# Value pooling as one VectorE reduction, and ScalarE work half a step later, in an attention + MoE + MoE kernel

## Chip, cores and metric

One core of a Trainium2 chip runs the whole program. The metric is the device time of one execution in microseconds (us). TensorE, VectorE, ScalarE, GpSimd and SyncE are called PE, DVE, ACT, POOL and SP in the rows, and PEld is TensorE's loading of weights.

## What is computed

Attention with pooled keys and values, then a gated MLP, then a routed mixture of eight experts. The part that the change touches is the attention and the first pieces of the MLP:

```python
B, H, S, D = 8, 8, 576, 64; pool = 8; Sp = S // pool              # 72 keys a head
k_p = k.reshape(B, H, Sp, pool, D).mean(axis=3)
v_p = v.reshape(B, H, Sp, pool, D).mean(axis=3)
scores = np.matmul(q, k_p.transpose(0, 1, 3, 2)) / np.sqrt(D)
attn = softmax(scores)
x = np.matmul(attn, v_p)                                           # tokens x 512 after a transpose
x = (silu(x @ w_gate) * (x @ w_val)) @ w_out                       # 512 -> 1536 -> 512
...                                                                # then 8 experts, top 1
```

## The kernel before

The kernel is written with a scheduling layer: functions issue instructions, and the layer decides, engine by engine, in which order they stand. What the author sets is a key for each piece of work (`at_key(key, function, ...)`); the pieces are called in the order of their keys, and the layer prefers earlier ones, but it moves instructions between pieces where it expects an engine to wait. The order that stands in the built program is therefore shown below apart from the diff.

**Attention stage (about the first 270 us).** There are 36 steps x of 128 query rows, nine for each pair of batches. For a step, `st_scores` makes scores on TensorE (sc), VectorE takes row maxima (nm, L335) and ScalarE the exponentials (e, L339). `st_norm` sums them on VectorE (sm, L345), adds a small number on GpSimd (L346), takes the reciprocal on VectorE (L347) and scales e on GpSimd (L348). `st_aT` transposes e on TensorE (aTp, L365) and copies it to `at`. There are four e tiles, e_100 to e_103, used in turn. `st_av` multiplies `at` with the pooled values vb on TensorE (xp, L380), ScalarE copies xp to xs (L382), and when four pairs of heads are done xs is stored to DRAM (xT).

**Pooling.** `k_pool` sums groups of eight keys by one VectorE reduction (kp, L294); the keys lie with the pool innermost. `v_pool` (L304) sums groups of eight values on GpSimd by three additions over 4, 2 and 1 of the eight, with the feature innermost; `v_finish` (L310, GpSimd) masks the result (vsum) by head into vb. Raw keys and values have two buffers each and are loaded by SP's queue, so a load waits until the pooling of two batches earlier is done.

**Units.** Parts of the MLP fill TensorE during attention. A unit u is 256 tokens; `u_load` reads them back from xT (ur), splits them into a high half (uh, ScalarE L217) and a low half (ul, GpSimd L218). `u_gemm1(u, f)` does 24 matmuls (ugv, L233), then tanh on ScalarE (ut, L236), two products on VectorE (L237, L238), a rounding on ScalarE (uhh, L241) and a difference on VectorE (uhl, L242). `u_gemm2` multiplies these by the output weights (acc, L253). There are 12 units with two f each. xp and ugv take their PSUM banks from one pair of buffers ("xg").

**Weights.** `w_split` (L143 to L157, ScalarE and VectorE) splits the first six weight tiles during the first 45 us. `load_bias` (L171 to L179, VectorE) runs once in the middle of the stage.

After the attention stage TensorE runs the MLP's matmuls (gv L457, x L480) and then the experts (L761, L780).

Of the kernel before, what the change touches and what calls it, by code (L numbers as in the profile page):

```python
# [8 lines left out]
F32 = mybir.dt.float32  # L9
# [4 lines left out]
ALU = mybir.AluOpType  # L14
AX = mybir.AxisListType
# [3 lines left out]
B, H, S, D = 8, 8, 576, 64  # L19
NT, DM, FF = B * S, H * D, 1536  # L20
E, F2 = 8, 1024
POOL = 8
# [49 lines left out]
def attention_moe_moe2(ctx: ExitStack, tc: tile.TileContext, q, k, v, w_gate, w_val, w_out,  # L72
                       modality, w_gate2, mbias, w12, consts, out):
    nc = tc.nc
    sy, gp, ve, ac, pe = nc.sync, nc.gpsimd, nc.vector, nc.scalar, nc.tensor
# [7 lines left out]
    def bank(tag, name):  # L83
        n = {"s": 2, "x": 4, "y": 2, "sc": 2, "at": 2, "xg": 2, "acc": 2}[tag]
        return psp[0].tile([128, 512], F32, tag=tag, bufs=n, name=name)
# [114 lines left out]
    ue = {}  # L200
# [22 lines left out]
    def u_gemm1(u, f):  # L223
        hi, lo = ue[u]["x"]
        w = wgv[f]
        p = bank("xg", "ugv")
        o = [p[:, 0:256], p[:, 256:512]]
        for j in range(2):
            n = 0
            for kk in range(4):  # L230
                ws = slice(j * 512 + kk * 128, j * 512 + (kk + 1) * 128)
                for a, x in ((0, hi), (0, lo), (1, hi)):
                    pe.matmul(o[j], lhsT=w[:, a, ws], rhs=x[kk], start=n == 0, stop=n == 11)  # L233
                    n += 1
        t = m1.tile([128, CH], F32, tag="t", bufs=2, name="ut")[:, 0:256]
        ac.activation(out=t, in_=o[0], func=ACTF.Tanh, scale=0.5)  # L236
        ve.scalar_tensor_tensor(out=t, in0=t, scalar=1.0, in1=o[0], op0=ALU.add, op1=ALU.mult)  # L237
        ve.tensor_tensor(out=t, in0=t, in1=o[1], op=ALU.mult)  # L238
        hh = m1.tile([128, CH], F32R, tag="hh", bufs=2, name="uhh")[:, 0:256]
        hl = m1.tile([128, CH], F32R, tag="hl", bufs=2, name="uhl")[:, 0:256]  # L240
        ac.copy(hh, t)  # L241
        ve.tensor_tensor(out=hl, in0=t, in1=hh.bitcast(F32), op=ALU.subtract)  # L242
        ue[u][f] = (hh, hl)
# [21 lines left out]
    with tc.tile_pool(name="p0", bufs=1) as p0, tc.tile_pool(name="ps0", bufs=1, space=PSUM) as ps0:  # L265
        psp[0] = ps0
        NE = 4
        vs_t = [p0.tile([128, 5, 64], F32, name=f"vsum{i}") for i in range(2)]
# [5 lines left out]
        for t in e_t:  # L274
            gp.memset(t[:, 576:640], 0.0)

        k_raw, v_raw, vb_t, q_t, at_t, xs_t, nm_t, sm_t = {}, {}, {}, {}, {}, {}, {}, {}

        def q_load(b):
            q_t[b] = p0.tile([128, 4, S], F32, tag="q", bufs=2, name="qt")  # L280
# [4 lines left out]
            sy.dma_start(out=k_raw[b].rearrange("p k r -> p (k r)"), in_=k[b])  # L285

        def v_load(b):
            v_raw[b] = p0.tile([128, 5, POOL, 64], F32, tag="vraw", bufs=2, name="vraw")
            sy.dma_start(out=v_raw[b].rearrange("p c r d -> p (c r d)"), in_=v[b])

        def k_pool(b):
            raw = k_raw.pop(b)
# [5 lines left out]
                              func=ACTF.Copy, scale=1.0 / 64)  # L298

        def v_pool(b):  # L300
            t = v_raw.pop(b)
            for w in (4, 2, 1):
                o = t[:, :, 0:w] if w > 1 else vs_t[b % 2].unsqueeze(2)
                gp.tensor_tensor(out=o, in0=t[:, :, 0:w], in1=t[:, :, w:2 * w], op=ALU.add)  # L304

        def v_finish(b):
            vb = p0.tile([128, 4, 2, 2, 64], F32, tag="vb", bufs=2, name="vb")
# [64 lines left out]

        def st_av(b, half, hp):
            n = 256 + 64 * half
            if hp == 0:
                xs_t[b, half] = p0.tile([128, 4, 320], F32, tag="xs", bufs=2, name="xs")
            xs = xs_t[b, half]
            xp = bank("xg", "xp")
            for w in range(2):
                pe.matmul(xp[:, :n], lhsT=vb_t[b][:, hp, w, :], rhs=at_t[b, half][:, hp + w, :], start=w == 0,  # L380
                          stop=w == 1)
            ac.copy(xs[:, hp, :n], xp[:, :n])  # L382
            if hp == 3:
                c0 = (b % 2) * S + half * 256
                ac.dma_start(out=xT_d[b // 2][:, :, c0:c0 + n], in_=xs[:, :, :n])
# [3 lines left out]
        def at_key(key, fn, *args):  # L389
            ev_.append((key, len(ev_), fn, args))  # L390

        as_, an, av, avs = 3.0, 1.7, 0.7, 0.45
        WS0, WSK, U0, UK = -3.9, 1.0, 5.0, 1.3
# [4 lines left out]
        for g in range(4):  # L398
            for b in (2 * g, 2 * g + 1):
                x = 9 * g + (4 if b % 2 else 0) - as_ - 1.0  # L400
                at_key(x, k_pool, b)
                at_key(x - 4.0, k_load, b)
                at_key(x - 3.9, q_load, b)
                x0 = 9 * g + (6 if b % 2 else 1) + av
                at_key(x0 - 1.5, v_finish, b)
                at_key(x0 - 3.0, v_pool, b)
                at_key(x0 - 5.5, v_load, b)
                x1 = 9 * g + (8 if b % 2 else 4) + av
                for hp in range(4):
                    at_key(x0 + hp * avs, st_av, b, 0, hp)  # L410
                    at_key(x1 + hp * avs, st_av, b, 1, hp)
        for n in range(3 * NW1 + 4):
            at_key((-7.8, -7.7, -5.0, -4.5)[n] if n < 4 else WS0 + (n - 4) * WSK + 0.1, w_load, n)
        for n in range(3 * NW1):
            at_key(WS0 + n * WSK, w_split, n)
        uitems = [(u, f) for u in range(NU) for f in range(EF)]
        def stored(i):
            return 9 * (i // 9) + (1, 1, 4, 4, 6, 6, 8, 8, 8)[i % 9] + av + 3 * avs

        x = U0 - UK  # L420
        for n, (u, f) in enumerate(uitems):
            x += UK
            if f == 0:
                xl = max(x - 1.7, stored(2 * u + 1) + 0.5)
                x = max(x, xl + 1.5)
                at_key(xl, u_load, u)
            if n == 8:
                at_key(xl - 0.1, load_bias, p0)
            at_key(x, u_gemm1, u, f)
            at_key(x + 0.9 * UK, u_gemm2, u, f)  # L430
        at_key(34.0, x_load, ORDER[0])
        at_key(36.0, x_load, ORDER[1])
# [492 lines left out]
```

## Time and profile before

| | |
|---|---|
| median of three runs | 1573.29 us (1572.08 to 1575.23) |
| the profiled execution | 1572.41 us |
| its span in the profile | 1570.5 us (1.9 us lie around it) |
| TensorE busy in the span | 1507.6 us, 96% |
| VectorE, ScalarE, GpSimd busy | 958.2, 644.1, 230.2 us |

TensorE is busy for 96% of the span, so a reader looks for the 4% where it is not, and for stretches in which its granted clock is below the full one.

### The profile page before, as it was taken

The numbers are of one execution on the slowest core, as the hardware profiler recorded it, in microseconds if no ns is written. First come the engines' busy times: TensorE is split into PE (matmuls) and PEld (weight loads), VectorE is DVE, ScalarE is ACT, GpSimd is POOL, SyncE is SP. The second block draws the span as 40 slices with busy tenths as digits, with TensorE's granted clock in tenths as the row PEclk, the third lists the DMA queues.
The fourth block names the chain that finished last, engine by engine and source line by source line (L and its number), as shares of the span: only waits on it lengthen the run. The fifth ranks groups of instructions, "written<-read, shape, count | busy, mean of one in ns | idle before, by whom it ended". The sixth has DMA issues, their size and how long they took to land. (4 is left out here: it accounts for less than half of the span.)

```text
span 1570.5 us, 23370 instructions
## 1 busy us (share of the span) xinstructions
PE 1507.6 (96%) x8664; PEld 1369.3 (87%) x8664; DVE 958.2 (61%) x2280; ACT 644.1 (41%) x1469; POOL 230.2 (15%) x249
## 2 busy tenths in 40 slices
PE   4788999999999999999999999999999999999996
PEld 3577888899999999999999999998888898988985
DVE  7556444699385763755736637277986666665660
ACT  4545766555422121121221211123556666656651
POOL 4676543000000000000000000001031211211101
PEclk9899999999999999999999999999999999999998
DMA  7686433444110301101011010007477666666520
GB/s 300 254 278 215 139 121 125 150 154 133 51 41 21 91 11 54 58 11 51 28 44 51 11 51 31 1 21 269 141 239 260 219 234 224 209 225 229 186 97 28
DMA packets 62219, 198.50 MB, mean 126 GB/s; under 512 B 7021, under 2 KB 28177, under 8 KB 49298
## 3 DMA queue, kind: packets, MB, share of 16 engines
q1 hardware_dynamic: 44114, 161.78, 30.8%
q0 software_dynamic: 6080, 19.42, 3.5%
q10 hardware_dynamic: 11904, 15.73, 2.8%
q8 instruction: 70, 1.15, 0.3%
q14 instruction: 51, 0.42, 0.1%
HBM read 162.28 MB, written 35.15 MB: 126 GB/s over the span
## 5 line engine op out<-in xcount | busy, mean ns | idle before, releaser
L457 PE MATMUL gv<-xh,gv 128*128 128x384 f32 x2048 | 546.5, 338 | 0.8 <-DVE t L462 0.8
L457 PEld LDWEIGHTS gv<-xh,gv 128*128 128x128 f32 x2048 | 373.4, 188 | 6.7 <-DVE t L462 1.2
L457 PE MATMUL gv<-xl,gv 128*128 128x384 f32 x1024 | 345.9, 338 | 0.0
L761 PEld LDWEIGHTS hp<-x2hl,w 128*128 128x128 f32 x1824 | 233.5, 188 | 10.9
L761 PE MATMUL hp<-x2hl,w 128*128 128x256 f32 x1824 | 242.5, 281 | 0.0
L480 PE MATMUL x<-wo,hh 128*128 128x512 f32 x768 | 242.1, 396 | 0.0
L457 PEld LDWEIGHTS gv<-xl,gv 128*128 128x128 f32 x1024 | 192.4, 188 | 5.2
L780 PE MATMUL po<-w,hh 128*128 128x512 f32 x608 | 193.1, 399 | 2.4 <-ACT hh L765 2.4
L510 DVE CUSTOM_DVE_ANT_0 junk<-row,w2g 128x512 bf16<-128x512 f32 x288 | 184.8, 682 | 1.6 <-ACT row L501 1.5
L461 ACT ACTIVATE t<-gv 128x384 f32<-128x384 f32 x128 | 63.1, 493 | 290.1 <-PE gv L457 290.0
L655 POOL DMA_INDIRECT xg<-x2d,gidx x38 | 39.5, 1039 | 953.9 <-DVE oidx L642 816.9
L732 DVE TENSOR_TENSOR w<-raw,w 128x512 fp32r<-128x512 f32 x152 | 106.1, 698 | 116.8 <-ACT w L730 112.8
L462 DVE SCALAR_TENSOR_TENSOR t<-t,gv 128x384 f32<-128x384 f32 x128 | 70.5, 551 | 171.8 <-ACT t L461 171.6
L480 PEld LDWEIGHTS x<-wo,hh 128*128 128x128 f32 x768 | 143.2, 189 | 23.5
L466 ACT CAST hh<-t 128x384 fp32r<-128x384 f32 x128 | 65.7, 513 | 235.2 <-DVE t L463 235.0
L480 PE MATMUL x<-wo,hl 128*128 128x512 f32 x384 | 152.4, 397 | 0.0
L730 ACT CAST w<-raw 128x512 fp32r<-128x512 f32 x152 | 94.1, 619 | 135.4 <-PE po L780 123.3
L780 PE MATMUL po<-w,hl 128*128 128x512 f32 x304 | 121.5, 400 | 0.1
L780 PEld LDWEIGHTS po<-w,hh 128*128 128x128 f32 x608 | 103.3, 188 | 16.7 <-ACT hh L765 2.6
L463 DVE TENSOR_TENSOR t<-t,gv 128x384 f32<-128x384 f32 x128 | 70.5, 551 | 54.7 <-PE gv L457 54.5
L734 DVE TENSOR_TENSOR w<-raw,w 128x512 fp32r<-128x512 f32 x152 | 103.7, 682 | 0.0
L467 DVE TENSOR_TENSOR hl<-t,hh 128x384 fp32r<-128x384 f32 x128 | 70.9, 554 | 39.9 <-ACT hh L466 39.7
(144 smaller groups left out, 1892.1 us busy)
## 6 DMA issues: line engine op xcount, KB each, us to landing
raw<-in_moe_w_dram SPq DMA_DIRECT2D x76, 1024.0 KB, 5.7
vraw<-in_v_dram SPq DMA_DIRECT2D x8, 1280.0 KB
x2d<-row SPq DMA_DIRECT2D x36, 256.5 KB, 3.4
kraw<-in_k_dram SPq DMA_DIRECT2D x8, 1152.0 KB, 5.9
qt<-in_q_dram SPq DMA_DIRECT2D x8, 1152.0 KB
xr<-xT SPq DMA_DIRECT2D x48, 192.0 KB, 2.4
w2g<-in_moe_w_gate_dram SPq DMA_DIRECT2D x12, 512.0 KB, 8.1
w2g<-in_moe_w_val_dram SPq DMA_DIRECT2D x12, 512.0 KB, 3.4
```

Source lines behind the costliest of these rows:

```text
L457: pe.matmul(p, lhsT=w[:, a, ws], rhs=x[kk], start=n == 0, stop=n == 11)
L462: ve.scalar_tensor_tensor(out=t, in0=t, scalar=1.0, in1=o[0], op0=ALU.add, op1=ALU.mult)
L463: ve.tensor_tensor(out=t, in0=t, in1=o[1], op=ALU.mult)
L466: ac.copy(hh, t)
L467: ve.tensor_tensor(out=hl, in0=t, in1=hh.bitcast(F32), op=ALU.subtract)
L480: pe.matmul(o, lhsT=hx[:, ts], rhs=w[:, f % 2, a, :], start=f == f0 and n == 0, stop=f == NF - 1 and n == 2)
L510: ve.tensor_tensor_reduce(out=junk, in0=r[:, 0:DM], in1=w2g[:, e, :], scale=1.0, scalar=0.0, op0=ALU.mult, op1=ALU.add, accum_out=L[:, tt, ...
L730: ac.copy(h1, src)
L732: ve.tensor_tensor(out=w[:, 1, 0:512].rearrange("p (k f) -> p k f", k=4), in0=src, in1=h1.bitcast(F32), op=ALU.subtract)
L734: ve.tensor_tensor(out=w[:, 1, 512:1024], in0=w2s, in1=w[:, 0, 512:1024].bitcast(F32), op=ALU.subtract)
L761: pe.matmul(hp, lhsT=w[:, a, c0:c0 + 128], rhs=x[:, kk, :], start=n == 0, stop=n == 11)
L780: pe.matmul(b["po"][tt], lhsT=hx[:, ts], rhs=w[:, a, 512:1024], start=f == 0 and n == 0, stop=f == 7 and n == 2)
```

## The change

It has two parts. `v_pool` becomes one VectorE reduction for each batch, over values which the host now lays out with the pool of eight innermost; the load moves the same bytes in rows of the same length. And the ScalarE work (with the VectorE work that follows it) of a unit and of xs gets functions and keys of its own: `u_act` stands 0.4 of a unit's pitch behind `u_gemm1`, and `st_xs` 0.3 of a step behind `st_av`; the reading back of tokens (`stored`) moves by the same 0.3.

```diff
@@ u_gemm1
+        ue[u]["o"] = o
+
+    def u_act(u, f):
+        o = ue[u].pop("o")
         t = m1.tile([128, CH], F32, tag="t", bufs=2, name="ut")[:, 0:256]
         ac.activation(out=t, in_=o[0], func=ACTF.Tanh, scale=0.5)
         ve.scalar_tensor_tensor(out=t, in0=t, scalar=1.0, in1=o[0], op0=ALU.add, op1=ALU.mult)
@@ v_load
-            v_raw[b] = p0.tile([128, 5, POOL, 64], F32, tag="vraw", bufs=2, name="vraw")
+            v_raw[b] = p0.tile([128, 5 * 64, POOL], F32, tag="vraw", bufs=2, name="vraw")
@@ v_pool
-            t = v_raw.pop(b)
-            for w in (4, 2, 1):
-                o = t[:, :, 0:w] if w > 1 else vs_t[b % 2].unsqueeze(2)
-                gp.tensor_tensor(out=o, in0=t[:, :, 0:w], in1=t[:, :, w:2 * w], op=ALU.add)
+            ve.tensor_reduce(out=vs_t[b % 2].rearrange("p c d -> p (c d)"), in_=v_raw.pop(b), op=ALU.add, axis=AX.X)
@@ st_av
-            xp = bank("xg", "xp")
-            for w in range(2):
-                pe.matmul(xp[:, :n], lhsT=vb_t[b][:, hp, w, :], rhs=at_t[b, half][:, hp + w, :], start=w == 0,
-                          stop=w == 1)
-            ac.copy(xs[:, hp, :n], xp[:, :n])
+            xp = xp_t[b, half, hp] = bank("xg", "xp")
+            for w in range(2):
+                pe.matmul(xp[:, :n], lhsT=vb_t[b][:, hp, w, :], rhs=at_t[b, half][:, hp + w, :], start=w == 0,
+                          stop=w == 1)
+
+        def st_xs(b, half, hp):
+            ...
+            ac.copy(xs[:, hp, :n], xp_t.pop((b, half, hp))[:, :n])
@@ keys
+                    at_key(x0 + hp * avs + 0.3, st_xs, b, 0, hp)
+                    at_key(x1 + hp * avs + 0.3, st_xs, b, 1, hp)
@@ stored
-            return 9 * (i // 9) + (1, 1, 4, 4, 6, 6, 8, 8, 8)[i % 9] + av + 3 * avs
+            return 9 * (i // 9) + (1, 1, 4, 4, 6, 6, 8, 8, 8)[i % 9] + av + 3 * avs + 0.3
@@ units
             at_key(x, u_gemm1, u, f)
+            at_key(x + 0.4 * UK, u_act, u, f)
             at_key(x + 0.9 * UK, u_gemm2, u, f)
```

On GpSimd, about the eighth step (the second e_103) and the second batch's values, before:

```order
L348 TENSOR_TENSOR e_101<-e_101,sm 128x576
L346 TENSOR_SCALAR sm<-sm 128x8
L348 TENSOR_TENSOR e_102<-e_102,sm 128x576
L304 TENSOR_TENSOR vraw<-vraw 128x5x256
L346 TENSOR_SCALAR sm<-sm 128x8
L304 TENSOR_TENSOR vraw<-vraw 128x5x128
L348 TENSOR_TENSOR e_103<-e_103,sm 128x576
L304 TENSOR_TENSOR vsum_97<-vraw 128x320
L310 TENSOR_TENSOR vb<-vsum_97,cc 128x4x128
```

and now:

```order
L349 TENSOR_TENSOR e_101<-e_101,sm 128x576
L218 TENSOR_TENSOR ul<-ur,uh 128x256 x2
L311 TENSOR_TENSOR vb<-vsum_97,cc 128x4x128 x2
L347 TENSOR_SCALAR sm<-sm 128x8
L349 TENSOR_TENSOR e_102<-e_102,sm 128x576
L347 TENSOR_SCALAR sm<-sm 128x8
L349 TENSOR_TENSOR e_103<-e_103,sm 128x576
```

The three additions are gone from between the scalings of e; the first unit's ul and the second batch's vb now stand ahead of the scaling of e_102, where they stood behind e_103.

On VectorE at the same place (line numbers of the changed file are higher by one to four), before:

```order
L335 TENSOR_REDUCE nm<-sc 128x4
L345 TENSOR_REDUCE sm<-e_101 128x8
L335 TENSOR_REDUCE nm<-sc 128x4
L347 RECIPROCAL sm<-sm 128x8
L369 COPY at_341<-aTp 128x64
L369 COPY at_441<-aTp 128x64
L294 TENSOR_REDUCE kp<-kraw 128x288
L335 TENSOR_REDUCE nm<-sc 128x4 x2
L345 TENSOR_REDUCE sm<-e_102 128x8
```

and now:

```order
L298 TENSOR_REDUCE kp<-kraw 128x288
L336 TENSOR_REDUCE nm<-sc 128x4 x2
L346 TENSOR_REDUCE sm<-e_101 128x8
L370 COPY at_337<-aTp 128x64
L370 COPY at_437<-aTp 128x64
L348 RECIPROCAL sm<-sm 128x8
L305 TENSOR_REDUCE vsum_97<-vraw 128x320
L336 TENSOR_REDUCE nm<-sc 128x4 x2
L346 TENSOR_REDUCE sm<-e_102 128x8
```

The key reduction kp moved ahead of the maxima nm and of the sum for e_101, and the new value reduction vsum stands ahead of the next maxima and of the sum for e_102.

On ScalarE, around the first xs of the first batch, before:

```order
L382 COPY xs<-xp 128x256
L371 COPY at_341<-aTp 128x4x128
L156 CAST gv_218<-wa 128x512
L339 ACTIVATE e_100<-sc,nm 128x72 x8
L382 COPY xs<-xp 128x256 x2
L156 CAST wo_183<-wa 128x512
L382 COPY xs<-xp 128x256
L339 ACTIVATE e_101<-sc,nm 128x72 x8
```

and now:

```order
L386 COPY xs<-xp 128x256 x2
L372 COPY at_337<-aTp 128x4x128
L156 CAST gv_216<-wa 128x512
L340 ACTIVATE e_100<-sc,nm 128x72 x8
L386 COPY xs<-xp 128x256 x2
L389 DMA xT_66<-xs 512x1x256
L156 CAST wo_183<-wa 128x512
L340 ACTIVATE e_101<-sc,nm 128x72 x8
```

Two copies to xs stand together ahead of e_100's exponentials instead of one, and the store follows the fourth copy at once. Behind the attention stage the order on all engines is the same as before.

## Rows read from the trace of the kernel before

**Rows 1.** The page: busy us of each engine, share of the span, instructions.

```profile
PE 1507.6 (96%) x8664; PEld 1369.3 (87%) x8664; DVE 958.2 (61%) x2280; ACT 644.1 (41%) x1469; POOL 230.2 (15%) x249
```

**Rows 2.** Stretches of 10 us: length, busy us by engine (instructions), PE clock, DMA share, GB/s.

```profile
20.00:30.00 10.00, 4.87 (x21) 4.02 (x21) 9.87 (x17) 5.71 (x21) 7.16 (x5) 1.00 0.80 326
...
60.00:70.00 10.00, 9.43 (x34) 6.92 (x35) 4.21 (x6) 3.69 (x12) 6.45 (x9) 0.61 0.60 221
...
90.00:100.00 10.00, 7.66 (x33) 6.20 (x34) 4.36 (x6) 2.81 (x10) 5.66 (x8) 0.66 0.63 217
...
140.00:150.00 10.00, 8.52 (x44) 7.72 (x45) 7.73 (x13) 2.59 (x9) 4.77 (x7) 0.83 0.13 42
150.00:160.00 10.00, 10.00 (x70) 9.30 (x69) 4.00 (x10) 6.78 (x24) 5.04 (x6) 1.00 0.42 147
```

**Rows 3.** TensorE's timeline where it waited: start, us, instructions, [idle before, releaser].

```profile
59.82 0.90 PE L365 MATMUL aTp<-cc,e 128*128 128x128 f32 x3 [4.22 <-POOL e L348]
...
91.74 0.90 PE L365 MATMUL aTp<-cc,e 128*128 128x128 f32 x3 [3.12 <-POOL e L348]
93.24 0.58 PE L233 MATMUL ugv<-ul,gv 128*128 128x256 f32 x1 [0.60 <-POOL ul L218]
...
134.75 0.63 PE L365 MATMUL aTp<-cc,e 128*128 128x128 f32 x4 [1.08 <-DVE at L369]
141.48 0.51 PE L253 MATMUL acc<-wo,uhl 128*128 128x512 f32 x1 [3.82 <-DVE uhl L242]
```

**Rows 4.** GpSimd's timeline ahead of the waits that end at 59.82 and 91.74.

```profile
53.84 2.89 POOL L304 TENSOR_TENSOR vraw<-vraw 128x1280 f32<-128x1280 f32 x1
...
57.13 1.53 POOL L304 TENSOR_TENSOR vraw<-vraw 128x640 f32<-128x640 f32 x1
58.62 1.15 POOL L348 TENSOR_TENSOR e<-e,sm 128x576 f32<-128x576 f32 x1
...
85.76 2.90 POOL L304 TENSOR_TENSOR vraw<-vraw 128x1280 f32<-128x1280 f32 x1 [0.96 <-DMA vraw<-in_v_dram]
...
89.05 1.53 POOL L304 TENSOR_TENSOR vraw<-vraw 128x640 f32<-128x640 f32 x1
90.54 1.15 POOL L348 TENSOR_TENSOR e<-e,sm 128x576 f32<-128x576 f32 x1
```

**Rows 5.** Timeline of GpSimd, then VectorE, ahead of the wait that ends at 141.48.

```profile
135.73 4.51 POOL L304 TENSOR_TENSOR vraw<-vraw 128x1280 f32<-128x1280 f32 x2
...
136.04 2.63 DVE L176 TENSOR_SCALAR biast<-biast 128x36 f32<-128x36 f32 x1
...
140.49 0.94 DVE L242 TENSOR_TENSOR uhl<-ut,uhh 128x256 fp32r<-128x256 f32 x1
141.35 0.17 DVE L176 TENSOR_SCALAR biast<-biast 128x36 f32<-128x36 f32 x1
```

**Rows 6.** Groups by line and shape, first 420 us: busy us, mean ns, idle before.

```profile
L304 POOL TENSOR_TENSOR vraw<-vraw 128x1280 f32<-128x1280 f32 x8 | 23.7, 2968 | 3.8 <-DMA vraw<-in_v_dram 3.8
...
L294 DVE TENSOR_REDUCE kp<-kraw 128x288 f32<-128x2304 f32 x8 | 20.3, 2543 | 3.7 <-DMA kraw<-in_k_dram 3.4 <-ACT kb L297 0.3
...
L304 POOL TENSOR_TENSOR vraw<-vraw 128x640 f32<-128x640 f32 x8 | 12.3, 1541 | 0.6
...
L304 POOL TENSOR_TENSOR vsum<-vraw 128x320 f32<-128x320 f32 x8 | 7.5, 940 | 0.4
```

**Rows 7.** VectorE's timeline while GpSimd added the first batch's values (25.96 to 32.19).

```profile
27.20 2.54 DVE L294 TENSOR_REDUCE kp<-kraw 128x288 f32<-128x2304 f32 x1
29.66 1.81 DVE L157 TENSOR_TENSOR gv<-wa,gv 128x512 fp32r<-128x512 f32 x1
...
39.59 0.69 DVE L157 TENSOR_TENSOR gv<-wa,gv 128x512 fp32r<-128x512 f32 x1 [1.28 <-ACT gv L156]
```

**Rows 8.** Waits of the first 420 us: engine and line, what it waited for, total us, times, longest.

```profile
ACT xs L382 <- PE xp L380: 23.3, 22, 6.2
...
PEld xp L380 <- ACT xs L382: 1.2, 2, 1.0
```

More of the change, by code (lines that the diff above doesn't have):

```diff
@@ L275, in attention_moe_moe2 @@
             gp.memset(t[:, 576:640], 0.0)
-        k_raw, v_raw, vb_t, q_t, at_t, xs_t, nm_t, sm_t = {}, {}, {}, {}, {}, {}, {}, {}
+        k_raw, v_raw, vb_t, q_t, at_t, xs_t, xp_t = {}, {}, {}, {}, {}, {}, {}
         def q_load(b):
@@ L287, in v_load @@
         def v_load(b):
-            v_raw[b] = p0.tile([128, 5, POOL, 64], F32, tag="vraw", bufs=2, name="vraw")
-            sy.dma_start(out=v_raw[b].rearrange("p c r d -> p (c r d)"), in_=v[b])
+            v_raw[b] = p0.tile([128, 5 * 64, POOL], F32, tag="vraw", bufs=2, name="vraw")
+            sy.dma_start(out=v_raw[b].rearrange("p x r -> p (x r)"), in_=v[b])
         def k_pool(b):
@@ L374, in st_av @@
             n = 256 + 64 * half
+            xp = xp_t[b, half, hp] = bank("xg", "xp")
[3 more added lines that the diff above has]
+        def st_xs(b, half, hp):
+            n = 256 + 64 * half
             if hp == 0:
@@ L904 @@
     arrays["in_v_dram"] = _np.ascontiguousarray(
-        a.reshape(B, 5, 128, POOL * D).transpose(0, 2, 1, 3).reshape(B, 128, 5 * POOL * D))
+        a.reshape(B, 5, 128, POOL, D).transpose(0, 2, 1, 4, 3).reshape(B, 128, 5 * POOL * D))
     for name in ("moe_w_gate", "moe_w_val"):
```

## The prediction

> **What bounds the kernel now.** I read first the page's line of busy time: TensorE works 1507.6 of 1570.5 us and no other engine passes 61% [rows 1]. So time can be won only where TensorE is idle or at a low clock, 62.9 us of idleness in all. Then the table of 10 us stretches [rows 2]. The change touches the attention stage, and behind it the order of all engines stays as it was, so the question is which stretches of that stage still have something to give. From 150 us on TensorE is busy 10.00 of 10 us at full clock, although VectorE works there only 4.00 and ScalarE 6.78: units fill it, and nothing that happens on another engine matters unless it empties TensorE's queue. What can be won or lost therefore lies ahead of 150 us. There the table shows two things to see: idle TensorE time, and three stretches with a mean granted clock of 0.61, 0.66 and 0.83. The clock has two levels, 1.2 and 2.4 GHz, so these means say that TensorE ran at 1.2 GHz for about 7.8, 6.8 and 3.4 us (twice the missing share of 10 us).
>
> Next the timeline of TensorE alone, for its waits [rows 3]. Each of the three slow stretches has a long wait at its head or just ahead of it: 4.22 us that end at 59.82, 3.12 that end at 91.74, 3.82 that end at 141.48. Two of them wait for GpSimd's scaling of e (L348). GpSimd's own timeline says why it is late [rows 4]: ahead of L348 at 58.62 stand two additions of values, 2.89 and 1.53 us, in the order of the queue; ahead of L348 at 90.54 stand 2.90 and 1.53. The third wait is for uhl on VectorE, and there VectorE was held [rows 5]: the same operation on 128x36 elements (L176) took 2.63 us while GpSimd added values (4.51 us from 135.73), and 0.17 us after it. So v_pool, which is not on any long chain by its busy time, makes the largest waits of the stage by standing in two queues.
>
> **The change, part by part.**
>
> *GpSimd loses the additions.* One batch costs 2.97 + 1.54 + 0.94 = 5.45 us, eight batches 43.5 us [rows 6]. GpSimd's remaining work does not change.
>
> *VectorE gets eight reductions.* The trace has no reduction of 2560 elements a partition, but kp is the same form with 2304, the pool innermost: 2543 ns [rows 6]. By size that is 2543 x 2560/2304 = 2.83 us, 22.6 us in all. A kp reduction took the same 2.54 us while GpSimd's additions ran beside it [rows 7], so I do not add a holding by GpSimd; the upper bound would be L157, which needed 1.81 us instead of 0.69 under the same additions [rows 7].
>
> The Trainium skill (VectorE: DVE Perf Modes, Rules for kernel authors) speaks against this part: it says that tensor_reduce on a hot path runs at the 1x rate only and is the slowest VectorE operation, so one should restructure. The kp row agrees with that rate, 0.91 elements per ns. Followed to the end, the rule makes VectorE the bound where it is already full, which is the second rival below.
>
> *The waits between 90 and 150 us.* At 91.74: without 2.90 + 1.53 us of additions in front, L348 runs some 4.4 us earlier, and the 3.12 us and the 0.60 us behind it are covered. At 134.75 and 141.48: without additions VectorE is not held; L176 alone gives back 2.63 - 0.17 = 2.46 us, and GpSimd's next work starts 4.5 us earlier. I count all of 3.12 + 0.60 + 1.08 + 3.82 = 8.6 us as won; the lower bound is nothing, should other waits take their places. With the idleness goes the low clock behind it: half of 6.8 and of 3.4 us, 5.1 us. This hangs on the clock falling because of these waits, which the order in the rows (wait first, low clock after) supports.
>
> *The start.* From 20 to 30 us VectorE is busy 9.87 of 10 [rows 2]: weights are split and nothing covers more work. Two reductions fall into the first 55 us. The first replaces additions that held VectorE: L157 gives back 1.81 - 0.69 = 1.1 us, so it costs 1.7. The second costs 2.83 in full, and it stands directly ahead of the maxima and the sum for e_102. Cost 4.5 us; bounds below.
>
> *The wait of 4.22 us at 59.82.* I do not count it as won. The additions ahead of e_103 are gone, but the built order puts the first unit's ul and both halves of vb ahead of e_102's scaling, kp ahead of e_101's sum and vsum ahead of e_102's. What was late because of GpSimd's additions is now late because of these. If it were won, it would bring 4.22 us and half of 7.8 us, 8.1 in all.
>
> *ScalarE's work later.* The instructions are the same. Copies to xs now stand in pairs behind other work, which costs nothing as long as TensorE does not need the bank back: ScalarE waited 23.3 us for xp, TensorE's weight loads 1.2 us for xs [rows 8]. Without that slack see the third rival. The read-back of tokens moves by 0.3 of a step, but the first store follows the fourth copy at once, and the first unit's matmuls stand two steps earlier in TensorE's order; I take zero for both.
>
> *New waits.* In the new order a reduction stands between the two products of a unit, so uhl is up to 2.83 us later there. Bounds: nothing, and 8 x 2.83 = 22.6 us. From 150 us on TensorE has no idleness although ScalarE and VectorE are used well, so such delays are mostly covered by the next unit; near the lower end I take 1.2 us.
>
> **Sum** against the profiled execution: 1572.4 - 8.6 - 5.1 + 4.5 + 1.2 = 1564.4 us. The median of the runs lies 0.9 us above that execution (1573.29 to 1572.41), so I forecast 1565.3 us. With the start's cost from 0 to 6.5 and the new waits from 0 to 4, this case alone runs from 1560 to 1570.
>
> **The rivals.**
>
> *The first wait is won too.* If GpSimd, freed of 5.45 us a batch, also passes ul and vb in time, another 8.1 us go: 1557 us, and with no cost at the start 1553. For it: without the additions in front, 4.4 us, the scaling of e_103 could start near 54 instead of 58.62 [rows 4]. Against it: the order just named. Chance 0.22.
>
> *The start eats the gain (no change).* If e_102's sum, scaling and transposes wait for kp (2.54), vsum (2.83), two ul and two vb (3.5 together), TensorE loses 8.8 us at the start instead of 4.5, with as much low clock behind it as the 4.22 us wait had (3.9 us) on top of what it has now: 8.6 + 5.1 - 8.8 - 3.9 - 1.2 is about zero, 1573 us. For it: VectorE at 9.87 of 10 in the start. Against it: TensorE has unit matmuls and scores to run there. Chance 0.20.
>
> *The banks (slower).* xp and ugv share two PSUM banks, and their emptying by ScalarE now stands later. There are 64 xp and 24 ugv, 88 hand-overs. The forecast's gain of 8.0 us is gone once a hand-over makes TensorE wait 0.09 us on average; at 0.15 us it is 13.2 - 8.0 = 5 us slower, 1578 us. For it: the work of a unit and of xs was given later keys with no other reason in the queue. Against it: ScalarE was the one that waited [rows 8], and the built order puts other matmuls between the pairs. Chance 0.13.
>
> **Chances and range.** The forecast has 0.45. A difference under 0.2%, about 3 us, is what a measurement of this kernel cannot tell from none. Faster: the forecast almost whole and the first rival, 0.66. Same: most of the second rival and an edge of the forecast, 0.18. Slower: the third and a part of the second, 0.16. The range from 1554 to 1576 us leaves out the far end of the first rival and the worse half of the third.
>
> **What the changed profile would show.** Right: no GpSimd instruction on raw values; eight vsum reductions of 2.8 us on VectorE; no TensorE wait above 2 us between 85 and 150 us, and a granted clock of 0.95 or more there; both L176 at 0.2 us. Wrong in the start: TensorE waits for e_102 or e_103 around 55 to 62 us longer than 4.2 us. Wrong in the banks: waits of TensorE for ScalarE's xs or ut that were not there. The prediction fails if the waits that go are replaced by others of the same length, since then the clock falls as before.

## Result and the profile after

The changed kernel takes 1561.14 us (median of four runs, 1560.46 to 1561.8), the kernel before beside it 1574.26 us (four runs, 1572.08 to 1575.8). The ratio is 0.9918, with a 95% interval from 0.99 to 0.9935: 13 us or 0.8% faster, within the range that was forecast and 4.2 us below the forecast itself. The profiled execution has a span of 1559.4 us, 11.1 less than before.

First the page's line of busy time of the changed kernel (columns as in [rows 1]) and, from its groups by line and shape of the first 420 us (busy us, mean ns, idle before), three VectorE groups.

```profile
PE 1504.5 (96%) x8664; PEld 1366.4 (88%) x8664; DVE 971.2 (62%) x2288; ACT 644.1 (41%) x1469; POOL 189.1 (12%) x225
```

```profile
L305 DVE TENSOR_REDUCE vsum<-vraw 128x320 f32<-128x2560 f32 x8 | 22.4, 2801 | 1.5 <-POOL vb L311 0.9 <-DMA vraw<-in_v_dram 0.6
L298 DVE TENSOR_REDUCE kp<-kraw 128x288 f32<-128x2304 f32 x8 | 20.3, 2534 | 3.2 <-DMA kraw<-in_k_dram 2.9 <-ACT kb L301 0.3
...
L176 DVE TENSOR_SCALAR biast<-biast 128x36 f32<-128x36 f32 x2 | 0.3, 175 | 0.0
```

GpSimd lost 41.1 us. VectorE got 22.4 us of reductions and yet its sum rose by 13.0 only: other operations became shorter now that GpSimd's additions no longer run beside them. Of the 9.4 us, `load_bias` gave 4.9 (L176 took 2.63 us for one in [rows 5], now 0.175), uhl 2.0 and the splits of gv 1.2. TensorE's busy time fell by 3.1 us with the same 8664 matmuls, which fits low clock that is gone; its idle time fell from 62.9 to 54.9.

Where that happened is seen in the stretches. First those of [rows 2], then two long ones, of the changed kernel, and the two long ones of the kernel before. In each row after the length: busy us and instructions of PE, PEld, DVE, ACT, POOL, then PE clock, DMA share, GB/s.

```profile
60.00:70.00 10.00, 9.51 (x70) 8.59 (x71) 8.25 (x13) 6.54 (x24) 4.63 (x8) 1.00 0.74 288
90.00:100.00 10.00, 7.35 (x50) 5.49 (x49) 5.32 (x11) 5.42 (x18) 5.61 (x8) 1.00 1.01 376
140.00:150.00 10.00, 10.00 (x66) 9.08 (x65) 6.91 (x11) 7.77 (x28) 3.61 (x5) 1.00 0.45 144
150.00:160.00 10.00, 10.00 (x65) 8.73 (x64) 3.45 (x9) 6.24 (x20) 4.66 (x7) 1.00 0.35 104
```

```profile
0.00:85.00 85.00, 60.46 (x303) 47.81 (x303) 66.83 (x111) 48.67 (x159) 32.11 (x49) 0.98 0.81 306
85.00:150.00 65.00, 59.01 (x363) 50.03 (x362) 43.20 (x75) 38.85 (x132) 26.67 (x35) 0.97 0.66 235
```

```profile
0.00:85.00 85.00, 54.87 (x262) 42.75 (x263) 55.30 (x100) 46.07 (x151) 46.44 (x55) 0.90 0.73 277
85.00:150.00 65.00, 54.74 (x318) 45.80 (x319) 38.79 (x64) 31.70 (x105) 46.69 (x43) 0.92 0.72 248
```

All three stretches of 10 us with a low clock are at 1.00 now. Both long stretches gained: TensorE is idle 24.5 instead of 30.1 us in the first and 6.0 instead of 10.3 in the second, and the clock rose in both. The start, which was forecast to lose, gained nearly as much as the stretch behind it (the estimate below).

TensorE's timeline of the changed kernel shows the waits that stand where those of [rows 3] stood, and the first matmul of a unit (L233):

```profile
55.05 0.39 PE L233 MATMUL ugv<-uh,gv 128*128 128x256 f32 x1 [1.00 <-ACT uh L217]
60.42 0.77 PE L366 MATMUL aTp<-cc,e 128*128 128x128 f32 x5 [1.84 <-POOL e L349]
...
97.17 0.76 PE L329 MATMUL sc<-kb,qt 128*128 128x144 f32 x4 [2.00 <-ACT e L340]
...
116.62 0.38 PE L233 MATMUL ugv<-uh,gv 128*128 128x256 f32 x1 [0.82 <-ACT uh L217]
117.42 0.39 PE L233 MATMUL ugv<-ul,gv 128*128 128x256 f32 x1 [0.42 <-POOL ul L218]
```

In the kernel before, the first unit's first matmul stood directly behind the wait of 4.22 us:

```profile
60.38 0.56 PE L233 MATMUL ugv<-uh,gv 128*128 128x256 f32 x1
```

The wait of 4.22 us is 1.84 us, with 1.00 ahead of it. The waits of 3.12 and 3.82 us are gone; instead there is one of 2.00 for the exponentials and a row of small ones for the units' inputs. GpSimd's timeline at that place (compare [rows 4]):

```profile
55.08 1.42 POOL L218 TENSOR_TENSOR ul<-ur,uh 128x256 fp32r<-128x256 f32 x2 [2.88 <-ACT uh L217]
56.45 2.06 POOL L311 TENSOR_TENSOR vb<-vsum,cc 128x512 f32<-128x512 f32 x2
58.60 0.23 POOL L347 TENSOR_SCALAR sm<-sm 128x8 f32<-128x8 f32 x1
59.22 1.15 POOL L349 TENSOR_TENSOR e<-e,sm 128x576 f32<-128x576 f32 x1 [0.39 <-DVE sm L348]
```

And the first ul in the kernel before:

```profile
61.67 1.41 POOL L218 TENSOR_TENSOR ul<-ur,uh 128x256 fp32r<-128x256 f32 x2
```

GpSimd now waits (2.88 us) for the first unit's input and makes its ul at 55.08; before, it came to ul at 61.67, behind the additions. So the first unit's matmuls start at 55.05 instead of 60.38, and they fill the time in which the scaling of e is still late. At the end of the stage the MLP's first matmul (gv) starts 11.7 us earlier; first the changed kernel, then the kernel before:

```profile
277.17 0.58 PE L464 MATMUL gv<-xh,gv 128*128 128x384 f32 x1
```

```profile
288.89 0.58 PE L457 MATMUL gv<-xh,gv 128*128 128x384 f32 x1
```

What follows takes as long as before, within 0.6 us.

For the stages an estimate helps: each matmul counted at the mean time of its kind in the full stretch from 150 to 273.7 us of before, scaled so that this stretch gives its own length. By it TensorE has done 6.0 us more work than before by 85 us, 7.3 more between 85 and 150, and 0.6 less between 150 and 270. The sum, 12.7, is 1.0 above the 11.7 us by which gv starts earlier; 2 us is about what the estimate is good for. By 50 us TensorE is not ahead yet (under 1 us behind), so the gain of the start stands between 50 and 85 us.

### The profile page after: what moved, and what is told of

Its sections match the earlier page's. It is cut to its first block, busy times and chain, and to the rows that moved or that the text cites. A ratio compares the mean times of both kernels' runs of the same rounds, so it can differ in the third digit from the quotient of the medians.

```text
span 1559.4 us, 23389 instructions
## 1 busy us (share of the span) xinstructions
PE 1504.5 (96%) x8664; PEld 1366.4 (88%) x8664; DVE 971.2 (62%) x2288; ACT 644.1 (41%) x1469; POOL 189.1 (12%) x225
## 4 chain that ended last, share of the span: by engine, by line
PE 85%; DMA 5%; DVE 4%; issue 3%; POOL 1%; ACT 1%; SPq 0%; POOLq 0%; ACTq 0%
PE gv L464 33%; PE x L487 17%; PE po L787 12%; PE hp L768 12%; PE ugv L233 3%; PE xp L378 3%; PE acc L257 2%; PE sc L329 1%; DMA x2d<-row 1%; DMA xT<-xs 1%; DMA ur<-xT 1%; PE tp L752 1%; PE aTp L366 1%; ACT e L340 1%; DMA w2g<-in_moe_w_gate_dram 1%
```

## Experiments

Ratios are to the kernel before, run beside each, with 95% intervals. Four questions: which part of the change does it; whether it is GpSimd's queue; what VectorE's added work costs; and what else bounds the start.

**One part alone.** Only the pooling (`v_pool` and its layout as in the diff, keys as before):

```diff
-                gp.tensor_tensor(out=o, in0=t[:, :, 0:w], in1=t[:, :, w:2 * w], op=ALU.add)
+            ve.tensor_reduce(out=vs_t[b % 2].rearrange("p c d -> p (c d)"), in_=v_raw.pop(b), op=ALU.add, axis=AX.X)
```

> Only the pooling moves to VectorE; the keys of ScalarE's work are those of before. Theory 1 (the additions in GpSimd's queue made TensorE's long waits): most of the 13 us, 1561 to 1566 us, and no TensorE wait on GpSimd's scaling above 2 us. Theory 2 (the later keys, through the order they give, made the gain): 1570 to 1575 us. Theory 3 (both are needed, as a reduction on VectorE needs the room that the later keys make): 1568 to 1572 us.

Measured: 1560.44 us, 0.9925 (0.9912 to 0.9937). One wait for the scaling above 2 us is left, 3.15 us at 22.39; it stands ahead of the first batch's pooling and in the kernel before as well (22.27). Only the keys (`u_act`, `st_xs`, `stored`), additions on GpSimd:

```diff
+            at_key(x + 0.4 * UK, u_act, u, f)
+                    at_key(x0 + hp * avs + 0.3, st_xs, b, 0, hp)
```

> Only the keys of a unit's and of xs's ScalarE work change; the values are still added on GpSimd. Theory 1: within 3 us of 1574, with waits of TensorE for GpSimd's scaling of 3 us and more left in the trace. Theory 2: 1561 to 1566 us. Theory 3: 1570 to 1576 us.

Measured: 1572.99 us, 1.0002 (0.9993 to 1.0011). The pooling makes the gain, and the keys alone make none that can be measured. Under the keys alone the first wait is even longer; TensorE's wait there, and GpSimd's timeline ahead of it:

```profile
60.60 0.90 PE L369 MATMUL aTp<-cc,e 128*128 128x128 f32 x3 [5.12 <-POOL e L352]
```

```profile
54.62 2.89 POOL L308 TENSOR_TENSOR vraw<-vraw 128x1280 f32<-128x1280 f32 x1
57.59 0.23 POOL L350 TENSOR_SCALAR sm<-sm 128x8 f32<-128x8 f32 x1
57.91 1.53 POOL L308 TENSOR_TENSOR vraw<-vraw 128x640 f32<-128x640 f32 x1
59.40 1.15 POOL L352 TENSOR_TENSOR e<-e,sm 128x576 f32<-128x576 f32 x1
```

The reader sees the picture of [rows 4] again: the scaling stands behind two additions. Then the pooling with one half of the keys each, first the units' key (`at_key(x + 0.4 * UK, u_act, u, f)`, xs at `st_av`'s key), then that of xs and `stored` (units as before):

> Pooling on VectorE and the later key for a unit's work; xs is copied at the old key and tokens are read back at the old key. If the later unit key is what fills TensorE about 55 us (the first unit standing two steps earlier), this is near the full change, 1561 to 1563 us; if the xs key does it, it is near the run with the pooling alone.

> Pooling on VectorE and the later key for xs and for the read-back; a unit's work at the old key. If the xs key fills TensorE about 55 us, near the full change, 1561 to 1563 us; if the unit key does it, near the run with the pooling alone. If both of these two runs stand near the pooling alone or near the full change, neither key matters by itself.

Measured: 1562.38 us, 0.9938 (0.9926 to 0.9951), and 1561.64 us, 0.9929 (0.9916 to 0.9942). With the changed kernel's 0.9918 these four intervals overlap: no half of the keys hides a gain or a loss that the other half takes back, as far as can be measured. TensorE's timeline of the pooling alone:

```profile
55.05 0.39 PE L233 MATMUL ugv<-uh,gv 128*128 128x256 f32 x1 [0.99 <-ACT uh L217]
62.98 0.39 PE L233 MATMUL ugv<-ul,gv 128*128 128x256 f32 x1 [1.24 <-POOL ul L218]
...
119.41 1.33 PE L325 MATMUL sc<-kb,qt 128*128 128x144 f32 x4 [2.84 <-ACT e L336]
```

So it is the pooling that brings the first unit forward to 55 us, and not a key. In the second stretch the wait is of another kind, 2.84 us for the exponentials. By the estimate above the pooling alone is 1.4 us ahead by 85 us and 9.4 between 85 and 150. Between its profiled execution and the changed kernel's some 4 us of the gain lie in another stretch, with the same total. One execution each does not show whether the keys move them there.

**Is it GpSimd's queue, or the single reduction?** The three additions as they were, on VectorE:

```diff
-                gp.tensor_tensor(out=o, in0=t[:, :, 0:w], in1=t[:, :, w:2 * w], op=ALU.add)
+                ve.tensor_tensor(out=o, in0=t[:, :, 0:w], in1=t[:, :, w:2 * w], op=ALU.add)
```

> The kernel before with its three additions of values issued on VectorE instead of GpSimd; layout, keys and everything else as before. Theory 1a (what counts is that the additions leave GpSimd's queue): 2240 elements of two-input work a batch, by the 682 to 700 ns of the 512-element rows 1.35 ns an element, 3.0 us a batch against the reduction's 2.8, so about the same as the pooling alone, 1559 to 1564 us. Theory 1b (the single reduction with the pool innermost counts, since two-input work on VectorE is held by GpSimd): additions stretched to 4 us and more, and 1566 to 1572 us.

Measured: 1563.56 us, 0.994 (0.9925 to 0.9955). Most of the gain comes with leaving GpSimd. That takes away two things at once, the additions' place in GpSimd's queue and the hold of VectorE beside them [rows 5]; no run takes away the one and keeps the other, so their shares are not shown. The groups by shape of its first 420 us price the additions on VectorE:

```profile
L304 DVE TENSOR_TENSOR vraw<-vraw 128x1280 f32<-128x1280 f32 x8 | 13.1, 1634 | 0.0
L304 DVE TENSOR_TENSOR vraw<-vraw 128x640 f32<-128x640 f32 x8 | 7.6, 955 | 0.0
L304 DVE TENSOR_TENSOR vsum<-vraw 128x320 f32<-128x320 f32 x8 | 5.1, 642 | 1.0 <-POOL vb L310 1.0
```

That is 3.23 us a batch against 2.80 for the reduction and 5.45 on GpSimd [rows 6]. The reduction's further 1.5 per mille lies within the overlap of the intervals.

**Finer pieces on GpSimd.** The same additions in three, two and one pieces:

```diff
+                for c in ((slice(0, 2), slice(2, 4), slice(4, 5)) if w == 4 else (slice(0, 3), slice(3, 5)) if w == 2 else (slice(0, 5),)):
```

> The kernel before, its additions on GpSimd cut into six pieces a batch (three, two and one) with the same work and the same engine. If what costs is GpSimd's total time ahead of the scaling of e and VectorE's being held beside it, nothing or little changes: 1571 to 1576. If it is the length of one block that nothing can pass, finer pieces let the scaling in between and much of the gain appears on GpSimd too: 1563 to 1568.

Measured: 1573.96 us, 1.0003 (0.9991 to 1.0014). Its GpSimd and TensorE timelines:

```profile
56.63 4.81 POOL L305 TENSOR_TENSOR vraw<-vraw 128x512 f32<-128x512 f32 x5
```

```profile
65.54 0.58 PE L233 MATMUL ugv<-ul,gv 128*128 128x256 f32 x1 [6.57 <-POOL ul L218]
...
113.17 0.58 PE L233 MATMUL ugv<-ul,gv 128*128 128x256 f32 x1 [4.05 <-POOL ul L218]
```

In the second batch five pieces stand in one row, 4.81 us, and what waits now is the first unit's ul, 6.57 us. In the fourth, fifth and seventh batches the scaling of e does stand between pieces; in the fourth:

```profile
94.67 1.68 POOL L305 TENSOR_TENSOR vraw<-vraw 128x256 f32<-128x256 f32 x2
96.31 1.15 POOL L349 TENSOR_TENSOR e<-e,sm 128x576 f32<-128x576 f32 x1
97.42 0.73 POOL L305 TENSOR_TENSOR vraw<-vraw 128x256 f32<-128x256 f32 x1
```

TensorE's wait of 3.12 us for the scaling [rows 3] is gone with that, and the time stays: behind the fifth batch's additions and its vb a unit's ul is late instead (4.05 us). So in this run it is not the length of one block that costs. Where the scaling passes, the same additions delay the next work behind them.

**Is VectorE held while GpSimd adds?** The kernel before, with `load_bias` moved out of the crowded stretch (its first operation from 129 to 198 us):

```diff
-            if n == 8:
+            if n == 16:
```

> The kernel before with the bias preparation eight units' halves later, when GpSimd adds no values any more; the additions stay on GpSimd. It takes away the holding of VectorE's four bias operations alone. If the 3.8 us wait of TensorE at 141 us and the low clock behind it come from that holding: 5 us faster, 1567 to 1569 us, and L176 at 0.2 us. If another wait takes the place, or the wait was no loss: 1571 to 1574 us with L176 at 0.2 us all the same.

Measured: 1570.81 us, 0.9982 (0.9972 to 0.9992), so 2.8 us, about half of the 5.5 us that the wait of 3.82 us with its clock had in the prediction. L176 took 0.18 and 0.72 us. VectorE's, GpSimd's and TensorE's timelines show what is left of the wait:

```profile
139.15 2.34 DVE L242 TENSOR_TENSOR uhl<-ut,uhh 128x256 fp32r<-128x256 f32 x1 [0.47 <-ACT uhh L241]
```

```profile
138.29 4.62 POOL L304 TENSOR_TENSOR vraw<-vraw 128x1280 f32<-128x1280 f32 x2
```

```profile
141.55 0.50 PE L253 MATMUL acc<-wo,uhl 128*128 128x512 f32 x1 [1.65 <-DVE uhl L242]
```

With L176 away uhl itself is the operation that is held: 2.34 us instead of the 0.42 that it takes later in this run, beside GpSimd's additions from 138.29 to 142.91. Here the hold fell on the operation that came to stand there. Where the 2.8 us were won is not shown: by the estimate this profiled execution is 3.3 us ahead between 85 and 150 us, but some 1.5 behind ahead of that and again after it, and its gv starts at 289.05, no earlier than before (288.89).

**What does VectorE's added work cost?** The pooling alone, each reduction made twice:

```diff
+            for _ in range(2):
+                ve.tensor_reduce(out=vs_t[b % 2].rearrange("p c d -> p (c d)"), in_=raw, op=ALU.add, axis=AX.X)
```

> The pooling alone (keys of before) with each value reduction done twice, which adds 22.4 us to VectorE. If the reductions of the start lie on the path in full, as the prediction's 4.5 us said, the first two batches cost 5.6 us again, and the later ones nothing: 1564 to 1568 us. If VectorE has room everywhere: 1560 to 1562 us. If VectorE is a bound in the whole stage up to 150 us: 1572 us and more.

Measured: 1567.39 us, 0.9963 (0.995 to 0.9976), against 0.9925 with one: 22.4 us more VectorE work cost about 6 us. The stretches of this run, then those of the pooling alone:

```profile
0.00:85.00 85.00, 53.34 (x239) 41.91 (x240) 64.00 (x98) 40.65 (x132) 26.73 (x42) 0.93 0.75 285
85.00:150.00 65.00, 58.18 (x372) 50.44 (x373) 52.56 (x80) 39.63 (x133) 26.57 (x36) 0.98 0.72 251
```

```profile
0.00:85.00 85.00, 56.59 (x272) 44.26 (x272) 63.72 (x104) 45.31 (x148) 30.32 (x46) 0.92 0.79 301
85.00:150.00 65.00, 61.02 (x382) 53.04 (x381) 42.40 (x80) 40.17 (x133) 26.00 (x36) 0.95 0.68 239
```

TensorE loses 3.25 us of busy time in the first 85 us and 2.84 between 85 and 150. Busy time also depends on the clock, so the work done says more: by the estimate TensorE has done about 5 us less by 85 us, 0.3 to 1.1 less between 85 and 150, and 2 to 3 less behind that; gv starts 8.2 us later in the profiled execution. In the first stretch VectorE's sum hardly rises (64.00 and 63.72), although it holds second copies. Between 20 and 60 us it goes from 34.1 to 38.0 of 40 us, nearly full, and so other work moves behind; vb comes late (TensorE waits 3.54 us for it at 38.23). The start costs about what was expected, and the later copies cost too, which was not. Whether that is their own cost or a delay handed on isn't settled.

**What else bounds the start?** VectorE and ScalarE split weights there [rows 2]. The pooling alone with a slower pace of splitting:

```diff
-        WS0, WSK, U0, UK = -3.9, 1.0, 5.0, 1.3
+        WS0, WSK, U0, UK = -3.9, 1.4, 5.0, 1.3
```

> The pooling alone (keys of before) with the weights' splits spread over 1.4 steps each instead of 1.0, to give VectorE room in the first 50 us, where it is 88 to 99% busy and TensorE idle for 10 of 30 us. If VectorE's load in the start is what TensorE waits for: 2 to 6 us faster than the pooling alone, 1554 to 1558 us. If the loads or the chain of a step set the start: 1559 to 1562 us. If the units then wait for their weights: slower, 1563 us and more.

Measured: 1557.11 us, 0.9907 (0.9892 to 0.9923). In the first 50 us TensorE is busy 29.96 instead of 27.28 us (about 1.5 us of work by the estimate), and the first transposes wait 1.18 us for e instead of 3.15. Then the same edit in the changed kernel and in the kernel before, and a pace of 1.8 in the pooling alone:

> The changed kernel whole, with the six weight tiles split at a slower pace as well (a tile every 1.4 steps instead of every 1.0). Theory A: the slower splitting gives VectorE and ScalarE room in the first 50 us, and the later keys stay worth nothing: then it stands where the pooling alone with slower splitting stood, at 1556 to 1559 us. Theory B: the later keys already took that room (the changed kernel's first transpose no longer waits for VectorE): then nothing is added and it stays at 1560 to 1562.

> The kernel before with nothing but the slower splitting of the weights (1.4 steps a tile). If the start's gain of about 3 us is one of VectorE's and ScalarE's room by itself, before gains the same: 1569 to 1571, a ratio near 0.998. If the room is only worth something once GpSimd's additions are gone (the wait of 4.22 us behind them takes back what is won ahead of it), before stays within 1 us: 1572 to 1574.

> Pooling on VectorE with the keys of before, the weights split every 1.8 steps. It sizes the start: if VectorE's fill there still costs, a further spread gains 1 to 3 us on 1557.1; if the weights' splitting then comes too late for the first unit, it loses, 1558 to 1562, and TensorE or the units wait for a split weight tile between 40 and 70 us.

Measured: 1558.17 us, 0.9908 (0.9895 to 0.9922); 1575.49 us, 1.0017 (1.0008 to 1.0027); 1557.81 us, 0.9902 (0.9887 to 0.9916). The three versions with slower splitting (0.9902 to 0.9908) lie below all four with pooling and the old pace (0.9918 to 0.9938); their intervals overlap with the nearest, so about 3 us of further gain is likely, not shown. The last, slower still, is within 1 us of the others, neither the gain nor the loss that was expected. In the kernel before the same edit costs 2.7 us, which neither expectation had. TensorE's waits there between 90 and 150 us:

```profile
93.61 0.69 PE L365 MATMUL aTp<-cc,e 128*128 128x128 f32 x2 [3.44 <-POOL e L348]
...
126.33 0.33 PE L365 MATMUL aTp<-cc,e 128*128 128x128 f32 x1 [2.50 <-DVE at L369]
...
139.11 0.63 PE L365 MATMUL aTp<-cc,e 128*128 128x128 f32 x4 [1.93 <-DVE at L369]
145.84 0.80 PE L253 MATMUL acc<-wo,uhl 128*128 128x512 f32 x1 [3.82 <-DVE uhl L242]
```

In its first 50 us TensorE is 3.6 us busier than before (29.50 and 25.92), which is about 1 us of work by the estimate; nothing of it is left by 85 us, and between 85 and 150 it falls 4.5 us behind. The waits for e and uhl are all there, and the two for `at`, 2.50 and 1.93 us, are longer than the 1.08 of [rows 3]. What is won ahead of GpSimd's additions is lost behind them, and more; why more is not shown.

## Why the prediction came out as it did

**What bounds the kernel: right.** Taking the additions off GpSimd makes the gain, as one reduction (0.9925) or as the same additions on VectorE (0.994). The keys alone leave the first wait (5.12 us) and the time; further on, waits of 2.74 us for ul and 3.44 for xs stand in place of the 3.12 and 3.82. How much of the cost is GpSimd's queue and how much the hold of VectorE is not shown.

**The size of the two operations: right.** 2.83 us was forecast for the reduction, 2.80 measured; eight take 22.4 instead of 22.6 us. It isn't held by GpSimd, as the kp row said.

**The waits between 90 and 150 us with their clock (13.7 us): right in kind, too large.** All four waits went and the clock from 85 to 150 rose from 0.92 to 0.97, but others took places: TensorE's idle time in that stretch fell by 4.3 us, against 8.6 counted as won. The estimate gives 7.3 us for the stretch, clock included. The condition "no wait above 2 us" held at its edge (2.00), and that of a clock of 0.95 held.

**New waits (1.2 us): too small, and of another kind.** They were sought at uhl, between the two products of a unit. But uhl became shorter (mean 550 ns, 633 before), and the new waits are for the exponentials (2.00) and for the units' inputs uh and ul (0.82, 0.42 and smaller). About 4 us between 85 and 150 us, by the idle times just named, and about 0.6 behind it. They are more than half of what was too much in the term above.

**The start (4.5 us lost): the step that failed.** It had the wrong sign: some 6 us were gained in the changed kernel's execution, and 1.4 in that of the pooling alone. Its price for VectorE's work was not absurd: doubling the reductions cost about 5 us of work in the first 85 us. What failed was the sentence on the wait of 4.22 us, that what had been late because of the additions would now be late because of ul, vb, kp and vsum in front of e. They do stand in front, and a wait of 1.84 us is left; but ul in front is the first unit's input, and it brings that unit's matmuls 5.3 us forward, which stand in the time of the old wait. The prediction had seen that these matmuls stand two steps earlier, and put it at zero without a reason. In the changed kernel's row the clock is 1.00 from 60 to 70 us instead of 0.61. The unit's place alone does not keep it there: in the pooling alone it starts at 55.05 too, a wait of 1.24 us for ul follows, and the clock of that stretch is 0.83. The order was read for what it delays and not for what it brings forward. That is the better part of the first rival, whose 1557 us lie as far from the result as the forecast does.

**The sum** was 4 us off because its errors point both ways: about 10 us too pessimistic in the start, about 6 too optimistic between 85 and 150.

**The other rivals fell.** The start didn't eat the gain. The banks gave no loss: the keys alone are at 1.0002, although under them ScalarE's copies do come late in one place (TensorE waits 3.44 us for xs at 119.87, in the changed kernel 0.35).

**The hold of VectorE: the mechanism is right, with half of its price.** Moving the held operation away gives 2.8 us of the 5.5, and the trace has the next one held in its place. The Trainium skill (GPSIMD Engine Reference, Key points) says that GpSimd shares its SBUF interfaces with VectorE, with contention for instructions of two SBUF inputs or in a two-port mode. The runs agree for uhl, with two inputs, 2.34 against 0.42 us, and for a reduction, with one, 2.54 against 2.53. L176, with one input, was held as well, 2.63 against 0.17; whether it ran in a two-port mode no run shows.

## What to carry over

When a built order is compared, ask of each instruction that moved forward which work it releases on the engine that bounds the kernel, as well as what it delays. A wait that goes is not won in full until one has looked for the next wait behind it: here 13.7 us counted came out as 7. Work that stands in an engine's queue ahead of a critical operation may be worth moving to a busier engine: 43.5 us off GpSimd for 22.4 us on VectorE gave 13 us, although VectorE is the fuller of the two.

## What was not expected of the hardware

- One VectorE reduction over 2560 elements (2.80 us) is shorter than three two-input additions over the same values (3.23 us), and about half of GpSimd's (5.45 us).
- A VectorE operation beside GpSimd's additions can be stretched to about the end of one addition, whatever its own size: L176 on 128x36 elements ended at 136.04 + 2.63 = 138.67 us, the addition, by the mean length of [rows 6], at 135.73 + 2.97 = 138.70 [rows 5]; uhl on 128x256, in the run with the later bias, at 141.49, the addition there at about 138.29 + 2.97 = 141.26. Reductions of 128x2304 run at their own 2.5 us.
- Slower splitting, which frees VectorE and ScalarE in the first 50 us, seems worth about 3 us without GpSimd's additions, and costs 2.7 us with them.
